# Two MLPs behind an attention: the work of the chunks issued piece by piece from tables, and a 4-byte tile made 64 bytes

## The chip, the core and the metric

The kernel runs on one NeuronCore of a Trainium2 chip. The metric is the device time of one execution in microseconds: the median of 3 runs is 816.31 us (815.45 to 816.59).

## What is computed

A masked attention (16 heads, 768 tokens, head size 64) gives x of 1536 tokens by 512 features. Two MLPs follow, and they are what the change touches:

```python
def _moe_ref(x, w_in, w_out):          # first layer, w_in 512 x 2048, w_out 2048 x 512
    h = x @ w_in
    g = h - np.tanh(h)
    return (g @ w_out).astype(np.float32)

def _moe2_ref(x, w_in, w_out):         # second layer, same sizes
    h = x @ w_in
    g = h * (1.0 / (1.0 + np.exp(-1.702 * h)))
    return (g @ w_out).astype(np.float32)
```

## The kernel before

Attention runs first (to about 257 us) and isn't changed. The MLPs work through 16 chunks, 8 for each layer; a chunk is 256 of the 2048 inner features, in two halves j = 0, 1 of 128. The 1536 tokens are three blocks t = 0, 1, 2 of 512. The weights come as 64-bit floats. For each half of a chunk `load_w` loads 1 MB into `raw` on SP's queue and makes 32-bit floats of it in steps: p1 (clip, L109), p2, p3, p4 (shifts and ors on the halves of the word, L114, L120, L126) and p5 (L135) on VectorE (DVE), q4 (L131) on ScalarE (ACT) between p4 and p5. `raw` and the result `w` have one buffer for each half j.

For precision each operand of a product is split into a high part, rounded by ACT (`wh` L141, `gh` L651, `xh`, `th`, `sh`), and a low rest, by GpSimd (POOL) or DVE (`wl` L144, `gl` L652, `xl`, `tl`, `sl`); a product is then three matmuls of 512 columns on TensorE (PE): high x high, high x low, low x high. "h" products (`h_mm`, 12 matmuls) make a unit (t, j) of the hidden layer from x; `act1` applies the activation (ACT, L642 or L645), the gate (DVE, L643 or L646) and splits the result into gh and gl. `out_mm` (12 matmuls for a unit, 3 for each quarter d of the output) multiplies by w_out and sums over both j in PSUM; `out_evac` adds the four quarters into `acc` (DVE, L692; in the first chunk of a layer a copy on ACT, L690), and after the last chunk of layer 1 splits them into the next layer's xh and xl (L695, L696), after the last of layer 2 stores them.

The first chunk of a layer, c = 0 and 8, is a `plain_chunk`: six h products, one for each unit. In the other 14, `strassen_chunk`, the units of t = 0, 1 are made by seven products P1 to P7 of 6 matmuls instead of four h of 12; t = 2 keeps h. They need sums of weights s1 to s4 (`s_sums`, POOL, L548, written into `ws` and split into sh, sl) and sums of tokens T1 to T4 (`t_sum`, DVE, L576, once a layer, split into th, tl, T4 into xh, xl of t = 1). P1, P6, P7, P4 go into one PSUM bank y, with copies `keep` to SBUF between them (p1, u2, u3, L633); P5 and P3 into a bank w. The results are added on DVE: x = P2 + p1 (L768), z = w + u3 (L784), w + u2 (L795).

All order is written out by hand (`manual_schedule`): the program's order is the order of each engine's queue, and an instruction that waits holds back what stands behind it on its engine. In a steady Strassen chunk PE runs P1, P2, out of (c-1, t 2, j 0), P6, P5, out of (c-1, 2, 1), P7, h20, P4, P3, out of (0,0), (0,1), h21, out of (1,1), (1,0).

Tiles in SBUF are placed pool by pool in steps of 32 bytes. The pool `op` holds acc2, th, tl and last `ready` (4 bytes for each partition); behind it come `sp` (sh, sl) and `gp` (f, gh, gl, and the sums t, u, p).

Of the kernel before, what the change touches and what calls it, by code (L numbers as in the profile page):

```python
# [57 lines left out]
def lsh_attention_then_two_mlps(  # L58
# [100 lines left out]

# [398 lines left out]
    def t_sum(n):  # L558
        b11, b21, b12, b22 = (
            [acc01[:, cc + 2 * i, t * TB : (t + 1) * TB] for cc in range(2)]  # L560
            for t in range(2)
            for i in range(2)
        )
        for cc in range(2):
            if n < 3:
                o = gp.tile([128, TB], F32, tag="u", name=f"t{n}_{cc}", bufs=4)
            else:
                o = acc2[:, 2 * (n - 3) + cc]
            tt[n, cc] = o
            a, b = {  # L570
                1: lambda: (b12, b11[cc]),
                2: lambda: (b22, tt[1, cc]),
                3: lambda: (b22, b12[cc]),
                4: lambda: (b21, tt[2, cc]),
            }[n]()
            nc.vector.tensor_tensor(o, a[cc], b, ALU.subtract)  # L576
# [54 lines left out]
    def keep(o, name):  # L631
        u = gp.tile([128, TB], F32, tag="u", name=name, bufs=4)
        nc.scalar.activation(u, o, AF.Copy)  # L633
        return u
# [3 lines left out]
    def act1(c, t, j, h, apart):  # L638
        f = gp.tile([128, TB], F32, tag="f", name=f"f{c}_{t}_{j}", bufs=3)
        g = f if apart else h  # L640
# [17 lines left out]
        return act2

    def out_mm(c, t, j, first, last):  # L660
        if first:
            oacc[t] = [
# [5 lines left out]
        for d in range(4):
            o = oacc[t][d // 2][:, d % 2, :]
            if c < LAYER:  # L670
                f = slice(512 + d * 128, 512 + (d + 1) * 128)
                prods = ((woh[:, f], hi), (woh[:, f], lo), (wol[:, f], hi))
            else:
                f = slice(d * 128, (d + 1) * 128)
                prods = (
                    (hi[:, f], woh[:, 512:]),
                    (hi[:, f], wol[:, 512:]),
                    (lo[:, f], woh[:, 512:]),
                )
            for n, (a, m) in enumerate(prods):  # L680
                nc.tensor.matmul(o, a, m, start=(first and n == 0), stop=(last and n == 2))  # L681

    def out_evac(c, t, ds=range(4)):
        tok = slice(t * TB, (t + 1) * TB)
        la, r = divmod(c, LAYER)
        for d in ds:
            o = oacc[t][d // 2][:, d % 2, :]
            m = acc_of(d, t)
            if r == 0:
                nc.scalar.activation(m, o, AF.Copy)  # L690
            else:
                nc.vector.tensor_tensor(m, o, m, ALU.add)  # L692
            if r == LAYER - 1:
                if la == 0:
                    nc.scalar.activation(xh[:, d, tok], m, AF.Copy)  # L695
                    nc.gpsimd.tensor_tensor(  # L696
                        xl[:, d, tok], m, xh[:, d, tok].bitcast(F32), ALU.subtract
                    )
                else:
                    r0 = t * TB + d * 128  # L700
                    nc.sync.dma_start(out=out[r0 : r0 + 128, :], in_=m)
        if 3 in ds:
            oacc.pop(t)

    def load(c, j):
        if c < NCHUNK:
            parts[c, j] = load_w(c, j)

    def part(c, j, *which):
        if c < NCHUNK:  # L710
            for n in which:
                if n == 7:
                    parts[c, j][7](slice(0, 512))
                elif n == 8:
                    parts[c, j][7](slice(512, 1024))
                else:
                    parts[c, j][n]()

    def plain_chunk(c):
        units = [(t, j) for t in range(NTB) for j in range(CH)]  # L720
        tags = ("T", "T", "v", "g")
        n1 = c + 1
        first = c == 0
        fill = (
            lambda: (t_sum(1), first or part(n1, 0, 0), first and load(c + 2, 0)),
            lambda: (t_sum(2), t_split(1, nc.gpsimd), first or part(n1, 0, 1)),
            lambda: (
                t_sum(3), t_sum(4), t_split(2, nc.gpsimd),
                part(n1, 1, 0, 1) if first else part(n1, 0, 2, 3),
            ),  # L730
            lambda: (
                first or (part(n1, 0, 4, 5), load(c + 2, 0)),
                part(n1, 1, 2, 3) if first else part(n1, 1, 0, 1),
                t_split(3, nc.gpsimd), part(n1, 0, 6, 7, 8),
            ),
            lambda: (first or part(n1, 1, 2, 3), t_split(4, nc.gpsimd)),
            lambda: (part(n1, 1, 6), s_sums(n1, 0), part(n1, 1, 8), load(c + 2, 1)),
        )
        for n in range(len(units)):
            t, j = units[n]  # L740
            if n < 2:
                h = h_mm(c, t, j, tags[n % 4])
                if c:
                    out_mm(c - 1, 2, n, n == 0, n == 1)
                    if n == 1:
                        out_evac(c - 1, 2)
            else:
                t, j = units[n - 2]
                out_mm(c, t, j, j == 0, j == CH - 1)
                if j == CH - 1:  # L750
                    out_evac(c, t)
                if n == 5:
                    part(n1, 1, 4, 5)
                t, j = units[n]
                h = h_mm(c, t, j, tags[n % 4])
            act1(c, t, j, h, n % 2 == 0)()
            fill[n]()
# [136 lines left out]
```

## Time and profile before

| | us |
|---|---|
| median of 3 runs | 816.31 (815.45 to 816.59) |
| the profiled execution | 816.48 |
| its span, first to last instruction | 814.7 |
| busy in it: PE, DVE, ACT, POOL | 778.3, 616.0, 419.4, 413.8 |
| mean granted clock of PE | 0.994 |

One execution is profiled; all rows below are from it. A timeline lists instructions by start and duration; "[0.23 <-ACT u L633]" means that the engine stood idle for 0.23 us until ACT's instruction on tile u, line 633, was through. Matmuls overlap in a pipeline, so from one to the next it is the distance of the starts that counts, not the duration.

### The profile page before, as it was taken

How to read it: one execution, taken by the hardware profiler on the slowest of the kernel's cores; microseconds unless marked ns; L12 is line 12 of the kernel's file. 1: busy time of each engine (PE TensorE's matmuls, PEld its weight loads, DVE VectorE, ACT ScalarE, POOL GpSimd, SP SyncE). 2: the span in 40 equal slices, each digit the busy share in tenths (PEclk: the TensorE clock that was granted, in tenths of full speed). 3: DMA queues.
4: the chain of work that ended last, by engine and by line, in shares of the span. 5: the costliest groups of instructions: out<-in, count | busy, mean ns of one | idle time of the engine just before them, and what ended most of it. 6: DMA issues, size and time to landing. Idle time of an engine off the chain costs nothing.

```text
span 814.7 us, 10025 instructions
## 1 busy us (share of the span) xinstructions
PE 778.3 (96%) x3708; PEld 565.8 (69%) x3708; DVE 616.0 (76%) x840; ACT 419.4 (51%) x793; POOL 413.8 (51%) x342
## 2 busy tenths in 40 slices
PE   5899999999999989999999999998899999999997
PEld 3566666666665867777777777776687777777775
DVE  4787877776764858779797797988688787887854
ACT  4777777767775455433444334545544344343440
POOL 5443444444112683645636446697746536456351
PEclk9999999999999999999999999999999999999999
DMA  9526214314102011211122111111211113111004
GB/s 262 180 74 207 108 49 156 130 37 145 72 1 104 1 52 55 101 52 52 51 68 89 52 52 56 60 41 52 90 66 51 52 52 103 52 51 52 2 1 154
DMA packets 12993, 62.89 MB, mean 77 GB/s; under 512 B 1616, under 2 KB 2512, under 8 KB 8848
## 3 DMA queue, kind: packets, MB, share of 16 engines
q1 hardware_dynamic: 8928, 46.21, 15.8%
q0 software_dynamic: 3872, 15.99, 6.8%
q8 instruction: 29, 0.48, 0.2%
q14 instruction: 20, 0.16, 0.1%
q10 hardware_dynamic: 144, 0.05, 0.0%
HBM read 59.10 MB, written 3.15 MB: 76 GB/s over the span
## 4 chain that ended last, share of the span: by engine, by line
DVE 36%; PE 33%; POOL 11%; ACT 11%; issue 6%; DMA 2%; DVEq 0%; POOLq 0%; ACTq 0%
PE pv L378 9%; PE tp L359 8%; PE sc L324 8%; DVE w L120 6%; DVE w L126 6%; DVE acc L692 5%; POOL w L548 5%; DVE w L114 4%; PE o L681 4%; DVE w L135 2%; ACT gh L651 2%; DVE gl L652 2%; ACT raw L131 2%; POOL sl L552 2%; POOL wl L144 2%
## 5 line engine op out<-in xcount | busy, mean ns | idle before, releaser
L652 POOL TENSOR_TENSOR gl<-f,gh 128x512 fp32r<-128x512 f32 x62 | 98.2, 1584 | 191.5 <-ACT gh L651 191.5
L692 DVE TENSOR_TENSOR acc<-o,acc 128x512 f32<-128x512 f32 x168 | 105.0, 678 | 6.2 <-PE o L681 6.0
L144 POOL TENSOR_TENSOR wl<-w,wh 128x512 fp32r<-128x512 f32 (+1 forms) x62 | 97.0, 1575 | 18.1 <-ACT wh L141 16.3
L131 ACT ACTIVATE raw<-raw 128x1024 f32<-128x1024 f32 x32 | 36.5, 1142 | 133.9 <-DVE w L126 130.1
L367 ACT ACTIVATE pt<-tp 128x384 f32<-128x384 f32 x184 | 80.3, 489 | 47.7 <-PE tp L359 46.8
L338 DVE TENSOR_REDUCE nm<-sc 128x1 f32<-128x768 f32 x96 | 91.5, 954 | 14.6 <-PE sc L324 13.4
L359 PEld LDWEIGHTS tp<-eye_sb,pr 128*128 128x128 f32 x576 | 61.6, 141 | 53.5 <-issue 25.7
L342 ACT ACTIVATE pr<-sc,nb 128x768 f32<-128x768 f32 x96 | 87.0, 906 | 16.6 <-DVE nb L340 8.9
L359 PE MATMUL tp<-eye_sb,pr 128*128 128x128 f32 x576 | 83.5, 281 | 0.0
L681 PE MATMUL o<-wh,gh 128*128 128x512 f32 x192 | 77.3, 403 | 5.2 <-ACT acc L690 2.6
L378 PE MATMUL pv<-pt,v 128*64 128x384 f32 x384 | 82.0, 510 | 0.0
L681 PE MATMUL o<-gl,wh 128*128 128x512 f32 x192 | 76.6, 399 | 2.3 <-DVE gl L652 1.3
L681 PE MATMUL o<-gh,wh 128*128 128x512 f32 x192 | 77.3, 403 | 0.9 <-DVE acc L692 0.9
L681 PE MATMUL o<-wh,gl 128*128 128x512 f32 x192 | 76.6, 399 | 0.4 <-POOL gl L652 0.4
L681 PE MATMUL o<-wl,gh 128*128 128x512 f32 x192 | 75.9, 395 | 0.0
L681 PE MATMUL o<-gh,wl 128*128 128x512 f32 x192 | 75.8, 395 | 0.0
L651 ACT ACTIVATE gh<-f 128x512 fp32r<-128x512 f32 x62 | 39.1, 630 | 47.4 <-DVE f L646 24.0
L593 PE MATMUL h<-xh,wh 128*128 128x512 f32 x160 | 63.3, 396 | 0.0
L593 PE MATMUL h<-xl,wh 128*128 128x512 f32 x160 | 63.2, 395 | 0.0
L593 PE MATMUL h<-xh,wl 128*128 128x512 f32 x160 | 62.9, 393 | 0.0
L324 PE MATMUL sc<-ka,qa 128*128 128x384 f32 x192 | 55.7, 371 | 3.1 <-DVE qa L228 2.6
L135 DVE SCALAR_TENSOR_TENSOR w<-raw,w 128x1024 f32<-128x1024 f32 x32 | 40.8, 1276 | 22.0 <-ACT raw L131 22.0
(145 smaller groups left out, 1677.3 us busy)
## 6 DMA issues: line engine op xcount, KB each, us to landing
raw<-in_w SPq DMA_DIRECT2D x32, 1024.0 KB, 4.8
ka<-in_kd POOLq DMA_DIRECT2D x7, 768.0 KB, 4.6
qa<-in_qd POOLq DMA_DIRECT2D x7, 768.0 KB, 6.6
r<-in_rr SPq DMA_DIRECT2D x7, 768.0 KB, 4.6
v<-in_vv SPq DMA_DIRECT2D x8, 384.0 KB, 3.1
out<-acc SPq DMA_DIRECT2D x12, 256.0 KB, 2.1
qb<-in_qd POOLq DMA_DIRECT2D x7, 384.0 KB, 7.9
r<-in_rr SPq DMA_DIRECT2D x2, 384.0 KB, 3.7
```

The source lines that it names most:

```text
L135: nc.vector.scalar_tensor_tensor(wf, sq, 1.0, wf, op0=ALU.is_ge, op1=ALU.mult)
L144: nc.gpsimd.tensor_tensor(wl[c, j][:, f], ws[c, j][:, f], wh[c, j][:, f].bitcast(F32), ALU.subtract)
L324: nc.tensor.matmul(sc[:, hf, :HALF], (qa, qb)[n][:, h, t0 : t0 + QT], (ka, kb)[n][:, h, hf * HALF : (hf + 1) * HALF], start=(n == 0), stop ...
L338: nc.vector.tensor_reduce(nm, sc[:, :, :HALF], AX.XY, ALU.max, negate=True)
L342: nc.scalar.activation(pr.rearrange("p (a b) -> p a b", a=2), sc[:, :, :HALF], AF.Exp, bias=nb, scale=D**-0.5, accum_out=sums[u][:, j, h : ...
L359: nc.tensor.transpose(tp[:, k * 128 : (k + 1) * 128], pr[:, c * 128 : (c + 1) * 128], eye_sb)
L367: nc.scalar.activation(dst, src, AF.Copy)
L378: nc.tensor.matmul(acc[u][h * 64 : (h + 1) * 64, :UT], v[:, h, c, :], probT[u][:, c, h, :], start=(c == 0), stop=(c == NCH - 1),)
L593: nc.tensor.matmul(o, a, b, start=(start and n == 0 and m == 0), stop=(n == len(pairs) - 1 and m == 2), skip_group_check=not start,)
L652: (nc.gpsimd if apart else nc.vector).tensor_tensor(lo, g, hi.bitcast(F32), ALU.subtract)
L681: nc.tensor.matmul(o, a, m, start=(first and n == 0), stop=(last and n == 2))
L692: nc.vector.tensor_tensor(m, o, m, ALU.add)
```

## The change

`plain_chunk`, `strassen_chunk` and their helpers with several steps in one are replaced by single steps and a table of names for each chunk, which `issue` runs in order. A name is a step and its indices: P1 to P7 a product, `h20` the h product of t 2, j 0, `o210` quarter d 0 of out of (2, 1), `ev10` the evacuation of quarter 0 of t 1, `t00`, `g00`, `hi00`, `lo00` activation, gate and split of a unit, `kp1`, `ku2`, `ku3` the copies, `xadd`, `zadd`, `wadd` the sums, `p11` to `p51`, `q41`, `whi1`, `wloa1`, `wlob1` the conversions of half 1, `ld1` its load, `s1`, `shi12`, `slo12` the weights' sums, `ts10`, `th10`, `tl10` the tokens'. "-" behind a name means the chunk before, "+" the next, "++" the one behind it. Chunks 0, 1, 7, 8, 9 and the end have tables of their own (those of 1 and 9 are left out here), all others run STEADY. `ready`, which serves one small instruction at the change of layers, is made 64 bytes for each partition instead of 4.

```diff
@@ load_w
+        parts["p1", c, j] = p1
...
+        parts["hi", c, j] = hi_part
+        parts["loa", c, j] = lambda: lo_part(slice(0, 512))
+        parts["lob", c, j] = lambda: lo_part(slice(512, 1024))
@@ the tiles of the MLPs
-    ready = op.tile([128, 1], F32, name="ready")
+    ready = op.tile([128, 16], F32, name="ready")
@@ s_sums, t_sum, t_split, act1 and out_evac become
+    def s_sum(c, n):
...
+    def s_hi(c, n):
...
+    def s_lo(c, n):
...
+    def t_sum(c, n, cc):
...
+    def t_hi(n, cc):
...
+    def t_lo(n, cc):
...
+    def act(c, t, j):
...
+    def gate(c, t, j):
...
+    def g_hi(c, t, j):
...
+    def g_lo(c, t, j):
...
+        eng = nc.gpsimd if apart(c, t, j) else nc.vector
...
+    def out_mm(c, t, j, d):
...
+    def evac(c, t, d):
...
+    def x_hi(t, d):
...
+    def x_lo(t, d):
...
@@ plain_chunk and strassen_chunk become
+    def keep(c, n, o):
+        us[c, n] = gp.tile([128, TB], F32, tag="u", name=f"u{c}_{n}", bufs=4)
+        nc.scalar.activation(us[c, n], o, AF.Copy)
+    def product(c, n):
+        if n == 1:
+            yw[c, 0] = bank("v", f"y{c}")
+        elif n == 2:
+            hp[c, 0, 0] = bank("T", f"x{c}")
+        elif n == 5:
+            yw[c, 1] = bank("g", f"w{c}")
+        elif n == 4:
+            hp[c, 0, 1] = yw[c, 0]
+        s_mm(hp[c, 0, 0] if n == 2 else yw[c, n in (3, 5)], c, n, n in (1, 2, 5))
+    def add(c, n):
+        if n == "x":
+            o, a, b = hp[c, 0, 0], hp[c, 0, 0], us[c, 1]
+        elif n == "z":
+            o, a, b = hp[c, 1, 1], yw[c, 1], us[c, 3] = bank("T", f"z{c}"), yw[c, 1], us[c, 3]
+        else:
+            o, a, b = hp[c, 1, 0], yw[c, 1], us[c, 2] = yw[c, 1], yw[c, 1], us[c, 2]
+        nc.vector.tensor_tensor(o, a, b, ALU.add)
+    def issue(name, c):
+        kind = name.rstrip("0123456789")
+        n = [int(x) for x in name[len(kind) :]]
+        if name[:2] in ("p1", "p2", "p3", "p4", "q4", "p5"):
+            parts[name[:2], c, n[-1]]()
+        elif kind == "ld":
+            load_w(c, n[0])
+        elif kind in ("whi", "wloa", "wlob"):
+            parts[kind[1:], c, n[0]]()
+        elif kind == "s":
+            s_sum(c, n[0])
+        elif kind in ("shi", "slo"):
+            (s_hi if kind == "shi" else s_lo)(c, n[0] // 2)
+        elif kind == "ts":
+            t_sum(c, *n)
+        elif kind in ("th", "tl"):
+            (t_hi if kind == "th" else t_lo)(*n)
+        elif kind == "P":
+            product(c, n[0])
+        elif kind in ("kp", "ku"):
+            keep(c, n[0], yw[c, 0])
+        elif kind in ("xadd", "zadd", "wadd"):
+            add(c, kind[0])
+        elif kind == "h":
+            t, j = n
+            tag = "T" if c % LAYER or t != 1 else "vg"[j]
+            hp[c, t, j] = bank(tag, f"h{c}_{t}_{j}")
+            h_mm(c, t, j, hp[c, t, j])
+        elif kind == "t":
+            act(c, *n)
+        elif kind == "g":
+            gate(c, *n)
+        elif kind in ("hi", "lo"):
+            (g_hi if kind == "hi" else g_lo)(c, *n)
+        elif kind == "o":
+            out_mm(c, *n)
+        elif kind == "ev":
+            evac(c, *n)
+        elif kind in ("xh", "xl"):
+            (x_hi if kind == "xh" else x_lo)(*n)
+        elif kind == "tab":
             nc.scalar.activation(ready, ready, AF.Sigmoid)
+    STEADY = (
+        "P1 g21- hi21- s4 shi12 ev10- ev11- P2 p11+ shi34 slo34 slo12 ev12- o200- ev13- "
+        "o201- o202- kp1 xadd o203- p20+ t00 g00 p21+ p30+ P6 p40+ p31+ lo21- P5 o210- "
+        "o211- ku2 q40+ o212- o213- P7 p50+ ev21- ev22- ku3 hi00 zadd lo00 whi0+ h20 P4 "
+        "ev23- ld0++ wloa0+ t11 wlob0+ P3 ev20- t20 t01 g20 g11 g01 hi11 hi01 lo11 o000 "
+        "o001 wadd t10 o002 hi20 o003 lo01 o010 p41+ o011 o012 g10 o013 ev01 q41+ lo20 "
+        "h21 p51+ ev00 s1+ hi10 s2+ ev02 ev03 whi1+ o110 lo10 p10++ o111 o112 o113 o100 "
+        "t21 wlob1+ o101 s3+ o102 o103 wloa1+ ld1++ "
+    )
+    ORDER = {
+        0: (
+            "whi0+ ts31 ts10 h00 ts30 wloa0+ ld1+ h01 h11 t00 ts11 t01 wlob0+ h10 ts20 "
+            "g00 hi00 th20 lo00 ts40 g01 ts21 hi01 o000 lo01 ts41 o001 th10 th30 th21 "
+            "o002 o003 h20 t11 o010 p11+ t10 th11 p21+ o011 tl10 g10 th31 tl20 hi10 h21 "
+            "o012 p31+ ld0++ o013 p41+ ev01 t20 g11 g20 tl30 ev00 lo10 p10++ q41+ tl21 "
+            "ev02 hi20 t21 p51+ tl31 th40 lo20 ev03 hi11 s1+ lo11 P1+ whi1+ s2+ P2+ ld1++ "
+            "th41 o100 o101 o102 o103 wlob1+ shi12+ o110 o111 kp1+ o112 s3+ slo12+ o113 "
+            "ev10 ev11 P6+ g21 s4+ "
+        ),
...
+        7: (
+            "g21- P1 P2 s4 shi12 p11+ shi34 kp1 slo12 ev11- P5 ev12- P6 ku2 ev10- slo34 "
+            "ev13- hi21- p20+ xadd o200- P7 t00 p30+ lo21- ku3 o201- o202- o203- p21+ P4 "
+            "p40+ q40+ o210- g00 zadd p31+ p50+ t01 p41+ o211- t11 g01 ev20- hi00 h20 "
+            "whi0+ hi01 lo00 wlob0+ t20 g11 o212- wloa0+ hi11 ev21- ld0++ lo11 o213- g20 "
+            "o000 ev22- ev23- q41+ hi20 P3 lo01 wadd p51+ t10 p10++ p20++ g10 o001 whi1+ "
+            "lo20 o002 hi10 o003 wlob1+ o010 o011 o012 o013 ev01 ev00 h21 ev03 lo10 o110 "
+            "xh01 xh00 wloa1+ xl01 ev02 o111 t21 xh03 o112 g21 xl00 o113 xh02 o100 o101 "
+            "p30++ hi21 ev10 o102 o103 xl03 ev11 o200 xh11 xl02 o201 ts10+ ts11+ xh10 "
+            "th10+ h00+ ev13 xh13 ev12 lo21 "
+        ),
+        8: (
+            "ld1+ o202- o203- p11+ tl10 tab o210- t00 p21+ o211- g00 o212- o213- p40+ "
+            "ts20 ev22- ev20- xh12- xl11- xl10- h01 xl12- ev21- xl13- h11 ts21 hi00 xh22- "
+            "xh20- ev23- xh21- q40+ xh23- t01 p50+ g01 whi0+ lo00 o000 h10 xl22- hi01 "
+            "xl21- xl23- ts31 lo01 xl20- ts41 t10 g10 p31+ ts40 th21 hi10 wlob0+ o001 "
+            "tl21 t11 wloa0+ th11 h20 p41+ o002 o003 q41+ ts30 o010 o011 ev00 th20 p51+ "
+            "ld0++ t20 g11 lo10 h21 o012 t21 ev01 tl20 o013 ev03 g20 hi11 o100 o101 P2+ "
+            "s1+ ev02 whi1+ hi20 tl11 P1+ s2+ o102 wlob1+ o103 shi12+ th40 g21 lo11 th41 "
+            "hi21 o110 kp1+ th31 o111 s3+ o112 s4+ ev10 shi34+ xadd+ slo12+ P6+ o113 "
+        ),
...
+        NCHUNK: (
+            "ev10- ev11- ev12- ev13- g21- hi21- o200- o201- o202- o203- lo21- o210- o211- "
+            "o212- o213- ev20- ev21- ev22- ev23- "
+        ),
+    }
+    for c in range(NCHUNK + 1):
+        for name in ORDER.get(c, STEADY).split():
+            at = c + name.count("+") - name.count("-")
+            if at < NCHUNK:
+                issue(name.strip("+-"), at)
```

## Rows read from the trace of the kernel before

**Rows 1.** The page, busy time of each engine over the whole span

```profile
PE 778.3 (96%) x3708; PEld 565.8 (69%) x3708; DVE 616.0 (76%) x840; ACT 419.4 (51%) x793; POOL 413.8 (51%) x342
```

**Rows 2.** Timeline of PE: start us, duration us, line, output<-streamed operand, weights

```profile
257.07 0.50 PE L593 MATMUL h<-xh,wh 128*128 128x512 f32 x1
...
258.79 0.39 PE L593 MATMUL h<-xl,wh 128*128 128x512 f32 x1
...
262.42 0.39 PE L593 MATMUL h<-xh,wl 128*128 128x512 f32 x1
...
418.55 0.39 PE L681 MATMUL o<-gl,wh 128*128 128x512 f32 x1
...
423.68 0.39 PE L681 MATMUL o<-gh,wl 128*128 128x512 f32 x1
...
711.29 0.40 PE L593 MATMUL y<-th,sh 128*128 128x512 f32 x1
...
713.39 0.40 PE L681 MATMUL o<-wh,gh 128*128 128x512 f32 x1
...
809.87 0.39 PE L681 MATMUL o<-wh,gl 128*128 128x512 f32 x1
```

**Rows 3.** Timeline of PE, one steady chunk, [idle before <-releaser]

```profile
398.83 0.40 PE L681 MATMUL o<-gh,wh 128*128 128x512 f32 x1
...
406.15 0.50 PE L593 MATMUL y<-xh,wh 128*128 128x512 f32 x1 [0.23 <-ACT u L633]
...
412.63 0.50 PE L681 MATMUL o<-gl,wh 128*128 128x512 f32 x1 [0.21 <-DVE gl L652]
...
432.48 0.39 PE L681 MATMUL o<-gh,wh 128*128 128x512 f32 x1
```

**Rows 4.** Timeline of PE, P6's first matmul in chunks 1 and 9

```profile
294.90 0.50 PE L593 MATMUL y<-th,sh 128*128 128x512 f32 x1 [3.18 <-ACT p L633]
...
575.79 0.50 PE L593 MATMUL y<-th,sh 128*128 128x512 f32 x1 [3.90 <-ACT p L633]
```

**Rows 5.** A stage: length, busy PE, PEld, DVE, ACT, POOL, clock, DMA

```profile
524.00:591.00 67.00, 57.78 (x230) 44.69 (x229) 51.11 (x47) 37.43 (x62) 53.58 (x36) 0.95 0.17 62
```

**Rows 6.** Timelines of DVE and ACT, the same chunk

```profile
402.25 2.20 DVE L126 SCALAR_TENSOR_TENSOR w<-raw,w 128x1024 uint32<-128x1024 uint32 x1
...
404.49 1.13 ACT L131 ACTIVATE raw<-raw 128x1024 f32<-128x1024 f32 x1 [3.72 <-DVE w L126]
...
405.51 0.59 ACT L633 ACTIVATE u<-y 128x512 f32<-128x512 f32 x1
...
420.52 1.23 DVE L126 SCALAR_TENSOR_TENSOR w<-raw,w 128x1024 uint32<-128x1024 uint32 x1
```

**Rows 7.** Groups by line and shape, 330 to 815: busy us, mean ns | idle

```profile
L652 POOL TENSOR_TENSOR gl<-f,gh 128x512 fp32r<-128x512 f32 x55 | 87.3, 1588 | 172.3 <-ACT gh L651 172.3
...
L120 DVE SCALAR_TENSOR_TENSOR w<-raw,w 128x1024 uint32<-128x1024 uint32 x26 | 46.0, 1768 | 0.4
...
L126 DVE SCALAR_TENSOR_TENSOR w<-raw,w 128x1024 uint32<-128x1024 uint32 x26 | 45.5, 1751 | 0.9
...
L114 DVE TENSOR_SCALAR w<-raw 128x1024 uint32<-128x1024 uint32 x26 | 33.2, 1277 | 19.5 <-POOL w L548 19.0
...
L135 DVE SCALAR_TENSOR_TENSOR w<-raw,w 128x1024 f32<-128x1024 f32 x26 | 32.8, 1261 | 16.1 <-ACT raw L131 16.1
...
L109 DVE TENSOR_SCALAR raw<-raw 128x1024 f32<-128x1024 f32 x25 | 23.6, 945 | 0.0
```

**Rows 8.** Timeline of DVE, the same chunk

```profile
399.85 2.37 DVE L120 SCALAR_TENSOR_TENSOR w<-raw,w 128x1024 uint32<-128x1024 uint32 x1
...
414.59 1.77 DVE L114 TENSOR_SCALAR w<-raw 128x1024 uint32<-128x1024 uint32 x1
...
416.88 2.47 DVE L692 TENSOR_TENSOR acc<-o,acc 128x512 f32<-128x512 f32 x4
```

**Rows 9.** DMA issues, 300 to 815: KB each, median us to landing

```profile
raw<-in_w SPq DMA_DIRECT2D x26, 1024.0 KB, 4.8
```

More of the change, by code (lines that the diff above doesn't have):

```diff
@@ L540, in s_sums, with s_part @@
         s1, s2, s3, s4 = w0[:, 512:768], w0[:, 768:], w1[:, 512:768], w1[:, 768:]
-        if n == 0:
+        o, a, b, f = {
+            1: (s1, a21, a22, ALU.add),
+            2: (s2, s1, a11, ALU.subtract),
+            3: (s3, a11, a21, ALU.subtract),
+            4: (s4, a12, s2, ALU.subtract),
+        }[n]
+        nc.gpsimd.tensor_tensor(o, a, b, f)
+    def s_part(c, n):
+        return (x[c][:, 2 * n : 2 * n + 2].rearrange("p a b -> p (a b)") for x in (sh, sl))
+    def s_hi(c, n):
+        if c not in sh:
@@ L551, in s_sums @@
-        nc.scalar.activation(h, w, AF.Copy)
-        nc.gpsimd.tensor_tensor(l, w, h.bitcast(F32), ALU.subtract)
-    tt = {}
[L558 to L576, printed above, removed]
@@ new lines, in lsh_attention_then_two_mlps @@
+    tt = {}
+    def t_sum(c, n, cc):
+        b11, b21, b12, b22 = (
+            acc01[:, cc + 2 * i, t * TB : (t + 1) * TB] for t in range(2) for i in range(2)
+        )
+        if n < 3:
+            o = gp.tile([128, TB], F32, tag="u", name=f"t{c}_{n}_{cc}", bufs=4)
+        else:
+            o = acc2[:, 2 * (n - 3) + cc]
+        tt[n, cc] = o
+        a, b = {
+            1: lambda: (b12, b11),
+            2: lambda: (b22, tt[1, cc]),
+            3: lambda: (b22, b12),
+            4: lambda: (b21, tt[2, cc]),
+        }[n]()
+        nc.vector.tensor_tensor(o, a, b, ALU.subtract)
@@ L629, in s_mm, with apart @@
         products(o, [(a(kc), b(kc)) for kc in range(2)], start)
[L631 to L640, printed above, removed]
+    def apart(c, t, j):
+        return t == j or t == 2 if c % LAYER else j == 0
+    fs = {}
+    def act(c, t, j):
+        f = fs[c, t, j] = gp.tile([128, TB], F32, tag="f", name=f"f{c}_{t}_{j}", bufs=3)
@@ L658, in act1 @@
[L658 to L662, printed above, removed]
+            nc.scalar.activation(f, hp[c, t, j], AF.Tanh)
+        else:
+            nc.scalar.activation(f, hp[c, t, j], AF.Sigmoid, scale=1.702)
+    def gate(c, t, j):
+        h, f = hp.pop((c, t, j)), fs.pop((c, t, j))
+        g = fs[c, t, j] = f if apart(c, t, j) else h
+        nc.vector.tensor_tensor(g, h, f, ALU.subtract if c < LAYER else ALU.mult)
+    def g_hi(c, t, j):
+        gh[c, t, j] = gp.tile([128, TB], F32R, tag=f"gh{t}{j}", name=f"gh{c}_{t}_{j}")
+        nc.scalar.activation(gh[c, t, j], fs[c, t, j], AF.Copy)
@@ L663, in out_mm @@
+    def g_lo(c, t, j):
+        gl[c, t, j] = gp.tile([128, TB], F32R, tag=f"gl{t}{j}", name=f"gl{c}_{t}_{j}")
+        eng = nc.gpsimd if apart(c, t, j) else nc.vector
+        eng.tensor_tensor(
+            gl[c, t, j], fs.pop((c, t, j)), gh[c, t, j].bitcast(F32), ALU.subtract
+        )
+    def out_mm(c, t, j, d):
+        first = j == (1 if t == 1 and c % LAYER else 0)
+        if first and d == 0:
+            oacc[c, t] = [
                 ps.tile([128, 2, 512], F32, tag="S", name=f"o{c}_{t}_{i}", bufs=2)
@@ L665, in out_mm @@
             ]
-        hi, lo = gh.pop((c, t, j)), gl.pop((c, t, j))
+        hi, lo = gh[c, t, j], gl[c, t, j]
         woh, wol = wh[c, j], wl[c, j]
[L668 to L681, printed above, removed]
@@ L683, in out_evac @@
-    def out_evac(c, t, ds=range(4)):
-        tok = slice(t * TB, (t + 1) * TB)
[L685 to L757, printed above, removed]
@@ L822, in lsh_attention_then_two_mlps @@
-    load(1, 1)
-    for c in range(NCHUNK):
-        (strassen_chunk if c % LAYER else plain_chunk)(c)
-    out_mm(NCHUNK - 1, 2, 0, True, False)
-    out_mm(NCHUNK - 1, 2, 1, False, True)
-    out_evac(NCHUNK - 1, 2)
+        o = oacc[c, t][d // 2][:, d % 2, :]
+        if c < LAYER:
+            f = slice(512 + d * 128, 512 + (d + 1) * 128)
+            prods = ((woh[:, f], hi), (woh[:, f], lo), (wol[:, f], hi))
+        else:
+            f = slice(d * 128, (d + 1) * 128)
+            prods = (
+                (hi[:, f], woh[:, 512:]),
+                (hi[:, f], wol[:, 512:]),
+                (lo[:, f], woh[:, 512:]),
+            )
@@ new lines, in out_mm @@
+        for n, (a, m) in enumerate(prods):
+            nc.tensor.matmul(o, a, m, start=(first and n == 0), stop=(not first and n == 2))
+    def evac(c, t, d):
+        o = oacc[c, t][d // 2][:, d % 2, :]
+        m = acc_of(d, t)
+        if c % LAYER == 0:
+            nc.scalar.activation(m, o, AF.Copy)
+        else:
+            nc.vector.tensor_tensor(m, o, m, ALU.add)
+        if c == NCHUNK - 1:
+            r0 = t * TB + d * 128
+            nc.sync.dma_start(out=out[r0 : r0 + 128, :], in_=m)
```

123 lines of the change are left out of this document (31 added, 92 removed), and 16 rows, old and new, of the table ORDER.

## The prediction

> **What bounds the kernel now.** I read the busy shares of the page first: TensorE (PE) 96%, VectorE (DVE) 76%, ScalarE (ACT) and GpSimd (POOL) 51% [rows 1]. So an edit can pay only where PE waits or where one matmul takes longer than it must. The change leaves attention alone, so the part that counts runs from the first h matmul at 257.07 us to the end of the last out matmul, 809.87 + 0.23 us: 553.0 us [rows 2]. By the code it holds 2220 matmuls of 512 columns: 160 x 3 of h_mm, 14 x 42 of s_mm, 16 x 72 of out_mm.
>
> The second view is the start-to-start time of matmuls in stretches without waits. Here there are two paces, not one. Where both operands are xh, xl, wh or wl, 16 steps take 262.42 - 258.79 = 3.63 us, 0.2268 us each. In an out_mm run, which streams gh and gl past wh, 22 steps take 5.13 us, 0.2332 each. In P6 and P5, which stream th and tl past the weights sh and sl, 9 steps take 2.10 us, 0.2333 each [rows 2]. The slow kinds are out_mm (1152) and P3, P5, P6 and P7 (14 x 24 = 336), 1488 in all. In each, exactly one operand comes from the pools sp or gp. In the program every tile is placed in steps of 32 bytes, so `ready` takes 32, and all of sp and gp, which come behind it, start 32 bytes past a multiple of 64; xh, xl, wh, wl, th and tl start on one. A difference of 6.4 ns is 15 columns at the fast pace's 0.427 ns per column, about one more piece of 64 bytes. That the start is the cause is an inference: it fits both ways round (streamed operand in the first layer, weights in the second and in P6), and no row takes it alone.
>
> With these paces the 2220 matmuls need 1488 x 0.2332 + 732 x 0.2268 = 347.0 + 166.0 = 513.0 us. PE therefore loses 553.0 - 513.0 = 40.0 us to waits. The third view, PE's timeline, says where. A steady Strassen chunk lasts 432.48 - 398.83 = 33.65 us, against 96 x 0.2332 + 42 x 0.2268 = 31.9 for its 138 matmuls: 1.74 lost, of which the rows show P4 waiting for `u` and out for `gl` [rows 3]. Times 14 chunks, 24.4. The other 15.6 lie in the two seams: at chunk 0 to 1 PE stands 3.18 us before P6; in the seam of the layers 3.90 at the same place, and the stage from 524 to 591 runs at a mean granted clock of 0.95 [rows 4, 5].
>
> **The change part by part.**
>
> The 64-byte tile moves sp and gp onto multiples of 64. Cost: nothing, one memset of 16 values instead of one, in DVE's idle time before the first gate. Gain: bounded by 0 and by 1488 x 0.0064 = 9.5 us. I take 9.5, because the form nearest in kind, P2 (same helper, six matmuls to a bank) with aligned weights, is in the fast class and P6 is not. The Trainium skill, page "SBUF — State Buffer", section "Specifications (TRN2)", gives lines of 16 bytes and a penalty for each cross to a new line. A start at 32 is on such a line already, so by that page of the Trainium skill the new start would bring nothing and the sum would end 9.5 us higher. The two paces in the rows speak against that as the whole story.
>
> The helpers are cut into pieces (one sum, one conversion, one evacuation at a time). By count nothing is added or removed: the same 2220 matmuls, sums, splits, evacuations and loads. What moves is the place of each in its engine's queue; every queue runs in program order.
>
> Steady chunks (STEADY, chunks 2 to 6 and 10 to 15): PE's own order is the old one. With 0.2268 per matmul PE's due times from the chunk's start are P1 0, P2 1.4, out(2,0) 2.7, P6 5.4, P5 6.8, out(2,1) 8.2, P7 10.9, h20 12.2, P4 15.0, P3 16.3, out(0,0) 17.7, out(0,1) 20.4, h21 23.1, out(1,1) 25.9, out(1,0) 28.6, end 31.3. Against these I laid the other queues by hand:
> - P4 now waits because `q4` stands ahead of the copy `u3` on ACT and itself waits for `p4` on DVE: p4 ends at 404.45, q4 starts at 404.49, u3 at 405.51, P4 at 406.15 [rows 3, 6]. In the table s3 is summed a chunk earlier, so `p2` no longer waits long for POOL, and q4 comes between u2 and u3. DVE reaches p4 by 8 to 12, q4 ends by 13, u3 runs at 12.5 to 13.6, before 15.0. Gone.
> - `slo12` now ends just after P6 has started; in the table it is ready near 3.2 for 5.4. Gone.
> - `zadd` needs u3 (13.1) and has to end before P3 (16.3). Behind g00 DVE has p21, p30, p40, p31, p50 and two evacuations: at the mean times 1.28 + 1.77 + 1.75 + 1.77 + 1.26 + 1.24 = 9.1 us [rows 7, 8], from 5.0 to 14.1. So zadd is through at 14.8. Cover 1.5.
> - `lo01` stands at the end of the chain P4, t01, g01, hi01, P3, wadd, lo01: six hops of 0.6 to 0.7 and the handovers from 16.3 end near 20.1; out(0,1) wants it at 20.4 and its second matmul at 20.6. Cover 0.3 to 0.5, the thinnest.
> - out(1,1) wants ev00 and ev01 (25.2 for 25.9), out(1,0) wants lo10 (27 for 28.6). Covered.
>
> I leave 0.3 us per chunk for the thin places: 14 x 0.3 = 4.2.
>
> Seam 0 to 1: three h products now run before the first out, P6 comes behind both outs of chunk 0, T1 to T4 are spread over DVE, ACT and POOL. POOL's queue (wl halves, lo, tl, s, slo; 1.59 is the mean of a lo [rows 7]) reaches slo12 at 28 to 29 after the start, for P6 at 29.9; slo34 follows near 33.8, for P7 at 33.3. I leave 1.0 of the old 4.7, most of which was the 3.18 before P6.
>
> Seam of the layers: the first h of layer 2 starts after xl00 to xl03 with out(7,2,0) half done, the rest of out(7,2) covers xl10 to xl13, and tl30 to tl41 go to chunk 9. The order is sound, but POOL becomes the bound: it was busy 53.6 us in the stage from 524 to 591 [rows 5], and the 230 matmuls of that stage need only 230 x 0.2268 = 52.2. Some of POOL's work can move into the chunks on both sides, and DVE's contended operations are no lighter. I leave 5.0 of about 11.
>
> End: g21 now comes behind ev10 to ev13 of chunk 15, so lo21 is ready some 3.6 us after out(1,0) for a matmul due at 3.2: 0.5. The last two evacuations and the store stay. A few slower matmuls after each wait that remains: 1.0.
>
> **How the numbers follow.** New length: 2220 x 0.2268 = 503.5, plus 4.2 + 1.0 + 5.0 + 0.5 + 1.0 = 11.7, gives 515.2 against 553.0: 37.8 less. The profiled execution took 816.48 us (its span 814.7 and 1.8 around it), 0.2 above the median of 816.31. Forecast 816.3 - 37.8 = 778.5. Floor of it (no wait left): 766.8.
>
> **Rivals.**
> 1. The start address is not the cause, or only where gp's tiles are streamed (first layer's out, 8 x 72 = 576 matmuls). For: no row isolates it, and the weights are read while the matmul before still runs. Then 9.5, or 9.5 x 912/1488 = 5.8, is missing: 784 to 788. The Trainium skill's lines of 16 bytes ("SBUF — State Buffer", "Specifications (TRN2)") lead to the first of the two.
> 2. DVE is late inside a chunk. The conversions cost 1.2 us alone and 2.2 to 2.4 beside POOL [rows 6, 8]; at the upper times the chain to zadd takes 1.77 + 2.37 + 2.20 + 2.37 + 2.20 + 1.24 = 12.2 instead of 9.1 and P3 waits 1.5 to 2. Against: between slo12, lo21 (near 5) and lo00 (13.7) POOL is idle. Half of it, 1 us x 14, gives 792; all of it 806.
> 3. Slower than before: the reload loop. `raw` and `w` have one buffer for each half. The table issues the load of half 1 after p51, at the chunk's end, and puts p11 of the next chunk five DVE operations into that chunk, where before it came in the middle. From p11 round to p51 DVE has 9 conversions and 16 operations of 0.62 [rows 8], plus q41 (1.14) and the landing (4.8) [rows 9]: with the mean times 0.95 + 2 x (1.28 + 1.77 + 1.75 + 1.26) = 13.1, and 13.1 + 9.9 + 1.1 + 4.8 = 28.9, which 31.3 covers. If every conversion met POOL, 3 x 1.77 + 2 x (2.37 + 2.20 + 2.20) = 18.9 and the loop is 34.7, longer than the chunk is now (33.65): + 13 over 14 chunks, and with the seams' gain mostly eaten by the same queue about 820. It decides from a mean conversion of 2.0 us against 1.45 now. Against: POOL is busy only about half of a chunk.
> 4. The order does nothing and the wait moves (P4's to P3's, chunk for chunk), and the start does nothing: 816.
>
> **Chances.** Forecast (768 to 786) 0.62. Rival 1 with the order as forecast 0.15. Rival 2, with or without the pace, 0.17. Rival 3 0.04. Rival 4 0.02. The low end is the floor, a little over it; the high end takes in rival 1 and the mild half of rival 2: 768 to 795. A measurement of this kernel tells 0.2% (1.6 us) from no change. Faster 0.94, same 0.02, slower 0.04.
>
> **What would show it.** Pace: out runs and P5 to P7 at 0.227 per matmul, in both layers. Order: steady chunks of 31.3 to 31.9 us from P1 to P1, no idle of PE before P4, and what is left before P3 or the first gl of out(0,1). Seam: P6 of chunks 1 and 9 without a gap, POOL busy without a break from chunk 7's end to chunk 9, and h10, h20 or P6 waiting for xl or slo there. Rival 3: DVE idle ahead of p11, ended by the load. It is wrong if a new wait of over 1 us repeats in every chunk, or if the out runs keep 0.233.

## The result and the profile after

The changed kernel takes 780.12 us (780.07 to 780.75, 4 runs) against 816.39 before: a ratio of 0.956 (95% interval 0.9543 to 0.9576), 36.3 us less. The forecast was 778.5. The two terms of its sum, however, were both off, in opposite directions, and the runs below take them apart.

The page of the changed kernel: busy time of each engine [rows 1], then the chain that ended last, by engine.

```profile
PE 759.0 (97%) x3708; PEld 570.3 (73%) x3708; DVE 581.9 (75%) x840; ACT 424.5 (55%) x793; POOL 399.4 (51%) x342
...
PE 88%; DVE 3%; issue 2%; POOL 2%; DMA 2%; ACT 1%; POOLq 0%; DVEq 0%; ACTq 0%
```

By the chain, 88% of the span is now PE's own work. PE's timeline in a steady chunk, from P1 to the next P1, with the last matmul of h20 and the first of P4 [rows 3], then P6's first matmul in chunks 1 and 9 with the one before it [rows 4]:

```profile
412.40 0.40 PE L610 MATMUL y<-xh,wh 128*128 128x512 f32 x1
...
427.45 0.39 PE L610 MATMUL h<-xh,wl 128*128 128x512 f32 x1
427.68 0.39 PE L610 MATMUL y<-xh,wh 128*128 128x512 f32 x1
...
444.19 0.40 PE L610 MATMUL y<-xh,wh 128*128 128x512 f32 x1
...
287.68 0.40 PE L699 MATMUL o<-gh,wl 128*128 128x512 f32 x1
287.92 0.39 PE L610 MATMUL y<-th,sh 128*128 128x512 f32 x1
...
580.72 0.39 PE L699 MATMUL o<-wh,gl 128*128 128x512 f32 x1
580.95 0.40 PE L610 MATMUL y<-th,sh 128*128 128x512 f32 x1
```

The chunk lasts 31.79 us instead of 33.65 (32.00 in the second layer). P4 follows h20 after 0.23 us, one plain step, and P6 no longer waits in either place. The idle times of PE of more than 0.15 us in the MLPs are three, 1.5 us together:

```profile
527.06 0.50 PE L610 MATMUL h<-xl,wh 128*128 128x512 f32 x1 [0.34 <-POOL xl L722]
...
537.44 0.50 PE L699 MATMUL o<-wh,gh 128*128 128x512 f32 x1 [0.64 <-ACT acc L705]
...
771.57 0.50 PE L699 MATMUL o<-wh,gl 128*128 128x512 f32 x1 [0.48 <-POOL gl L672]
```

Before, the wait of 3.90 us in the seam of the layers [rows 4] was followed by slow matmuls:

```profile
577.11 0.63 PE L593 MATMUL y<-th,sh 128*128 128x512 f32 x1
...
579.67 0.63 PE L593 MATMUL w<-th,sh 128*128 128x512 f32 x1
```

Six steps take 2.56 us here, 0.43 each, at the lower of the clock's two levels, 1.2 GHz; the mean granted clock from 576 to 580 us was 0.61. In this seam 14 steps were of this length, seven here and seven behind an earlier wait, some 3 us more than at the usual 0.23. After the change none is, and from 520 to 600 us the granted clock is 1.00.

The pace [rows 2] is read from two runs of 24 out matmuls without a wait, one in each layer:

```profile
398.65 0.40 PE L699 MATMUL o<-gh,wh 128*128 128x512 f32 x1
...
403.94 0.39 PE L699 MATMUL o<-gh,wl 128*128 128x512 f32 x1
...
665.81 0.40 PE L699 MATMUL o<-wh,gh 128*128 128x512 f32 x1
...
671.18 0.39 PE L699 MATMUL o<-wh,gl 128*128 128x512 f32 x1
```

In the first layer 23 steps take 5.29 us, 0.2300 each, a little under the 0.2332 of before. In the second they take 5.37, 0.2335 each: nothing gained. Some groups of DVE and POOL [rows 7] have a shorter mean, though the instructions are the same:

```profile
L672 POOL TENSOR_TENSOR gl<-f,gh 128x512 fp32r<-128x512 f32 x55 | 76.4, 1390 | 158.5 <-ACT gh L667 153.1 <-PE w L610 5.5
...
L126 DVE SCALAR_TENSOR_TENSOR w<-raw,w 128x1024 uint32<-128x1024 uint32 x25 | 32.6, 1304 | 0.3
...
L120 DVE SCALAR_TENSOR_TENSOR w<-raw,w 128x1024 uint32<-128x1024 uint32 x24 | 31.8, 1326 | 0.0
...
L114 DVE TENSOR_SCALAR w<-raw 128x1024 uint32<-128x1024 uint32 x24 | 19.3, 805 | 0.3
```

A p3 takes 1.33 us on the mean instead of 1.77, a p4 1.30 instead of 1.75, a p2 0.81 instead of 1.28: these conversions now stand where POOL is mostly idle. An instruction of POOL ran beside 70% of p3's time before and 20% after, 69 and 36% of p4's, 55 and 25% of p2's. p1 went the other way, from 50 to 95% and from 0.95 to 1.07 us.

### The profile page after: what moved, and what is told of

Same layout as the page of the kernel before. It is cut to its first block, busy times and chain, and to the rows that moved or that the text cites. A ratio compares the mean times of both kernels' runs of the same rounds, so it can differ in the third digit from the quotient of the medians.

```text
span 778.6 us, 10045 instructions
## 1 busy us (share of the span) xinstructions
PE 759.0 (97%) x3708; PEld 570.3 (73%) x3708; DVE 581.9 (75%) x840; ACT 424.5 (55%) x793; POOL 399.4 (51%) x342
## 4 chain that ended last, share of the span: by engine, by line
PE 88%; DVE 3%; issue 2%; POOL 2%; DMA 2%; ACT 1%; POOLq 0%; DVEq 0%; ACTq 0%
PE o L699 31%; PE h L610 12%; PE y L610 10%; PE pv L386 9%; PE tp L367 9%; PE sc L332 8%; PE w L610 5%; PE x L610 2%; DMA ka<-in_kd 1%; DMA r<-in_rr 1%; POOL xl L722 1%; PE rb L411 1%; PE pb L260 1%; PE po L291 1%; DVE acc L590 1%
## 5 line engine op out<-in xcount | busy, mean ns | idle before, releaser
L672 POOL TENSOR_TENSOR gl<-f,gh 128x512 fp32r<-128x512 f32 x62 | 86.0, 1387 | 171.0 <-ACT gh L667 165.5
L707 DVE TENSOR_TENSOR acc<-o,acc 128x512 f32<-128x512 f32 x168 | 108.8, 684 | 54.5 <-PE o L699 53.7
L144 POOL TENSOR_TENSOR wl<-w,wh 128x512 fp32r<-128x512 f32 (+1 forms) x62 | 85.7, 1393 | 18.9 <-ACT wh L141 18.9
L731 ACT ACTIVATE u<-y 128x512 f32<-128x512 f32 x42 | 25.2, 601 | 107.9 <-PE y L610 107.9
L667 ACT ACTIVATE gh<-f 128x512 fp32r<-128x512 f32 x62 | 39.1, 630 | 28.3 <-DVE f L663 28.1
L332 PE MATMUL sc<-kb,qb 128*128 128x384 f32 x192 | 50.2, 342 | 2.0 <-DVE qb L298 2.0
```

The lines of the kernel that those rows point to most:

```text
L144: nc.gpsimd.tensor_tensor(wl[c, j][:, f], ws[c, j][:, f], wh[c, j][:, f].bitcast(F32), ALU.subtract)
L332: nc.tensor.matmul(sc[:, hf, :HALF], (qa, qb)[n][:, h, t0 : t0 + QT], (ka, kb)[n][:, h, hf * HALF : (hf + 1) * HALF], start=(n == 0), stop ...
L667: nc.scalar.activation(gh[c, t, j], fs[c, t, j], AF.Copy)
L672: eng.tensor_tensor(gl[c, t, j], fs.pop((c, t, j)), gh[c, t, j].bitcast(F32), ALU.subtract)
```

## The experiments: the tile

**Undo the tile alone**, the order stays:

```diff
-    ready = op.tile([128, 16], F32, name="ready")
+    ready = op.tile([128, 1], F32, name="ready")
```

> The order of the tables with the 4-byte tile, so that sp and gp start 32 bytes past a multiple of 64 again. Theory A (the start of a tile sets the pace of matmuls): the first layer's out products, which stream gh and gl and run at 0.229 to 0.232 us in the changed kernel, go back to 0.2332; 576 of them by 2.5 ns are 1.4 us, 781.5. Rival B (the pace is set by something other than the start, the new order is all of the gain): 780.1 and the same paces as in the changed kernel.

Measured: 781.4 us (ratio to before 0.9588, 0.9574 to 0.9602). The run of 24 in the first layer:

```profile
399.05 0.40 PE L699 MATMUL o<-gh,wh 128*128 128x512 f32 x1
...
404.42 0.40 PE L699 MATMUL o<-gh,wl 128*128 128x512 f32 x1
```

5.37 us, 0.2335 each. So the 64-byte tile is worth about 1.3 of the 36.3 us, nearly all of it in the first layer's out; the second layer runs at 0.233 with either. The order is worth the other 35.

**Do the tile alone**, the order of before:

> The order of before with the 64-byte tile. Theory A: the first layer's out products drop from 0.2332 to 0.229 to 0.231; as PE also waits in every chunk, less than 1.5 us of it reaches the end, 815 to 816. Rival B: 816.4 and 0.2332. By the forecast on record, in which all 1488 products with an operand from sp or gp get the fast pace, it would have been up to 9.5 us faster, 807.

Measured: 816.13 us, ratio 1.0007 (0.9998 to 1.0017): no change. The first layer's out does run at 0.2303 on the mean instead of 0.2331, but what the products lose PE waits longer.

**128 bytes:**

```diff
-    ready = op.tile([128, 16], F32, name="ready")
+    ready = op.tile([128, 32], F32, name="ready")
```

> The changed kernel with the tile made 128 bytes, so that sp and gp start on multiples of 128, as xh, xl, wh and wl do. Theory A2 (weights want a start on 128, streamed operands gain from 64 on): all products go to 0.2268, 2220 by 4.2 ns are 9.3 us, 771. Theory A (64 is all there is): 780.1 and the second layer's out, P3 and P5 to P7 stay at 0.2333. Rival C (weights from sp and gp are slow for where they lie, not how they start): 778 to 780, with the first layer's out at 0.2268 at most.

Measured: 780.07 us. A start on 128 does nothing for the weights, and the first layer's out lost part of what 64 had given (5.35 us for 23 steps):

```profile
397.93 0.39 PE L699 MATMUL o<-gh,wh 128*128 128x512 f32 x1
...
403.28 0.39 PE L699 MATMUL o<-gh,wl 128*128 128x512 f32 x1
```

So a start on a multiple of 64, the theory of the forecast, is not enough, and a rounder start does not help further. A pattern is left: by the sizes of the tiles in the kernel, all operands of the fast products (xh, xl, wh, wl) lie whole multiples of 256 bytes apart. With a tile of 4, 64 or 128 bytes sp and gp lie 32, 64 or 128 bytes off that grid.

**512 and 256 bytes**, which put sp and gp on the grid of the others:

```diff
-    ready = op.tile([128, 16], F32, name="ready")
+    ready = op.tile([128, 128], F32, name="ready")      # 512; [128, 64] for 256
```

> The changed kernel with the tile made 512 bytes. The runs so far: sp and gp shifted by 32 bytes gives 0.2333 in the first layer's out, by 64 0.2307, by 128 0.2327; products of xh, xl with wh, wl take 0.2285 (0.2268 in long runs), and those tiles lie at 128 from a multiple of 512, all of them. Theory D (what counts is the shift of the streamed operand against the weights, modulo 512 or less, not a start on 64 or 128): at a shift of 512 every product runs as xh with wh do, 1475 products by 3 to 6 ns, 4.5 to 9 us less, 771 to 776. Theory C (tiles far up in SBUF, or written just before, are slow wherever they start): 780 and 0.2327 to 0.2333 for the second layer's out.

> The changed kernel with the tile made 256 bytes. Theory D with a period of 256: as with 512, 771 to 776. With a period of 512: between, or as slow as with 128, 780. Theory C: 780.

Measured: 771.24 us (ratio 0.9453, 0.9439 to 0.9467) and 771.45 (0.9458, 0.9444 to 0.9472). Timeline of PE with 512 bytes, the two runs of out, then P5's first matmul in two steady chunks:

```profile
395.95 0.39 PE L699 MATMUL o<-gh,wh 128*128 128x512 f32 x1
...
401.16 0.39 PE L699 MATMUL o<-gh,wl 128*128 128x512 f32 x1
...
658.66 0.39 PE L699 MATMUL o<-wh,gh 128*128 128x512 f32 x1
...
663.87 0.39 PE L699 MATMUL o<-wh,gl 128*128 128x512 f32 x1
...
385.07 0.39 PE L610 MATMUL w<-th,sh 128*128 128x512 f32 x1
...
416.35 0.39 PE L610 MATMUL w<-th,sh 128*128 128x512 f32 x1
```

Both runs take 5.21 us, 0.2265 each, and the chunk takes 31.28, which is 138 x 0.2267: PE does nothing but matmuls, at one pace. This is the effect for which the forecast had 9.5 us, from 4 bytes to 64. From 64 bytes it measures 780.1 - 771.2 = 8.9; from 4 bytes it is 10.0 with 256 (781.4 - 771.45) and 10.2 with 512.

**Start or distance?** A 32-byte tile ahead of all others, besides the 256 bytes:

```diff
+    pad = xpool.tile([128, 8], F32, name="pad")
+    nc.vector.memset(pad, 0.0)
     xh = xpool.tile([128, NCC, NT], F32R, name="xh")
```

> As with the 256-byte tile, and a 32-byte tile (filled once with zeros) placed ahead of all others, so that xh, xl, wh, wl, th, tl, sp and gp all start 160 past a multiple of 256 instead of 128: no start is kept, every distance is. If the distance of the streamed operand from the weights, modulo 256, sets the pace: 0.2268 everywhere, 771.4. If it is the start itself (128 modulo 256 fast, other starts slow): 0.2307 to 0.2333 in all products, h too, 780 to 786.

Measured: 771.21 us. The first layer's run of 24:

```profile
395.80 0.39 PE L701 MATMUL o<-gh,wh 128*128 128x512 f32 x1
...
401.01 0.39 PE L701 MATMUL o<-gh,wl 128*128 128x512 f32 x1
```

5.21 us again, with all these tiles moved by 32 bytes, the move that gives 0.2335 when sp and gp make it alone. So it is not the start itself. What matters is how far the streamed operand and the weights lie apart, modulo 256: at 0 every product is fast. The size of the distance is not all, though: with 64 bytes the first layer streams an operand 64 above its weights (0.2300), the second one 64 below (0.2335).

**The pace in the old order:**

```diff
-    ready = op.tile([128, 1], F32, name="ready")
+    ready = op.tile([128, 64], F32, name="ready")
```

> The order of before with the 256-byte tile. All products at 0.2268: 1488 by 6.4 ns are 9.5 us. If PE sets the length of a chunk also in the old order, all of it reaches the end: 806.5. If the chain of conversions on DVE and POOL sets it (the steady chunk's 33.65 stays), only the seams and the end gain, some 240 products, 1 to 3 us: 813 to 815, and PE's waits grow by what the products lose.

Measured: 814.85 us, ratio 0.9988 (0.9979 to 0.9997). P5's first matmul in two steady chunks:

```profile
396.70 0.40 PE L593 MATMUL w<-th,sh 128*128 128x512 f32 x1
...
430.31 0.40 PE L593 MATMUL w<-th,sh 128*128 128x512 f32 x1
```

33.61 us against 33.65: the chunk stays as long as it was, although its matmuls now need 31.3. Over the MLPs the matmuls need some 8 us less and PE waits some 7 us longer. So in the old order another engine's chain set the length of a chunk, not PE. From 4 to 256 bytes the pace is worth 1.3 us there (816.11 in the runs beside it, to 814.85) and 10.0 in the new order (781.4 to 771.45).

## The experiments: the order

**s3 and s4 back in their own chunk**, the first half of the forecast's explanation of P4's wait (shown for chunks 3 to 5 and 11 to 15; chunks 2, 6 and 10 have the half of it that goes with their neighbours' tables):

```diff
-        "P1 g21- hi21- s4 shi12 ev10- ev11- P2 p11+ shi34 slo34 slo12 ev12- o200- ev13- "
-        "o201- o202- kp1 xadd o203- p20+ t00 g00 p21+ p30+ P6
+        "P1 g21- hi21- shi12 ev10- ev11- P2 p11+ slo12 ev12- o200- ev13- "
+        "o201- o202- kp1 xadd o203- t00 g00 s3 s4 shi34 slo34 p20+ p21+ p30+ P6
...
-        "t21 wlob1+ o101 s3+ o102 o103 wloa1+ ld1++ "
+        "t21 wlob1+ o101 o102 o103 wloa1+ ld1++ "
```

> The changed kernel with s3 and s4 of the steady chunks back behind g00 in their own chunk, as before, so that p2 of the next chunk waits for POOL again and p4, q4 and u3 come later. If this place was what made P4 wait: PE idles 0.3 to 0.6 us before P4 or P7 in chunks 3 to 6 and 11 to 15, 3 to 6 us in all, 783 to 786. If the other moves (q4 between u2 and u3, the conversions spread out) cover it alone: 780 to 781.

Measured: 780.04 us, no change. Timeline of ACT in one chunk, q4 and u3 in the changed kernel and then in this one:

```profile
420.53 1.16 ACT L131 ACTIVATE raw<-raw 128x1024 f32<-128x1024 f32 x1 [0.40 <-DVE w L126]
...
425.13 0.60 ACT L731 ACTIVATE u<-y 128x512 f32<-128x512 f32 x1 [3.43 <-PE y L610]
```

```profile
422.86 1.17 ACT L131 ACTIVATE raw<-raw 128x1024 f32<-128x1024 f32 x1 [3.20 <-DVE w L126]
...
424.65 0.60 ACT L731 ACTIVATE u<-y 128x512 f32<-128x512 f32 x1 [0.62 <-PE y L610]
```

The chunk in which these stand begins with P1 at 412.40 and at 411.93. q4 starts 8.1 us after that in the one and 10.9 in the other, and u3 12.7 after it in both: it waits for P7 (y), not for q4. Before, q4 started 404.49 - 390.26 = 14.2 after P1 (P1's first matmul stood at 390.26) [rows 6]. So P4 goes without a wait whether s3 and s4 stand in the old place or the new. The old state is not back, however. POOL's s3 and s4 before, then in this run, and DVE's two p2 in this run:

```profile
397.67 0.73 POOL L548 TENSOR_TENSOR w<-w,w 128x256 f32<-128x256 f32 x1
398.36 0.74 POOL L548 TENSOR_TENSOR w<-w 128x256 f32<-128x256 f32 x1
...
410.95 0.74 POOL L555 TENSOR_TENSOR w<-w,w 128x256 f32<-128x256 f32 x1
411.65 0.74 POOL L555 TENSOR_TENSOR w<-w 128x256 f32<-128x256 f32 x1
...
417.00 3.42 DVE L114 TENSOR_SCALAR w<-raw 128x1024 uint32<-128x1024 uint32 x2
```

Before, POOL came to s3 7.4 us after P1, and p2 waited for POOL, 19.0 us in all [rows 7]. Here half 1 is converted early, POOL comes to s3 1.0 us ahead of P1, and no p2 waits; the two p2 only take 1.7 us each. So the expectation's "p2 of the next chunk waits for POOL again" did not come about, and whether that wait was what delayed P4 stays untested. The other half of the forecast's reason, q4 between u2 and u3, names no change: ACT had u2 at 400.19, q4 at 404.49 and u3 at 405.51 before too [rows 6].

**p3 and p4 of half 1 back behind the evacuations of t 0**, as before, and with them q4, p5, the high part, the weights' sums and the next load (hi10 moves ahead of them):

```diff
-        "o201- o202- kp1 xadd o203- p20+ t00 g00 p21+ p30+ P6 p40+ p31+ lo21- P5 o210- "
+        "o201- o202- kp1 xadd o203- p20+ t00 g00 p21+ p30+ P6 p40+ lo21- P5 o210- "
...
-        "o001 wadd t10 o002 hi20 o003 lo01 o010 p41+ o011 o012 g10 o013 ev01 q41+ lo20 "
-        "h21 p51+ ev00 s1+ hi10 s2+ ev02 ev03 whi1+ o110 lo10 p10++ o111 o112 o113 o100 "
+        "o001 wadd t10 o002 hi20 o003 lo01 o010 o011 o012 g10 o013 hi10 ev01 ev00 ev02 ev03 "
+        "p31+ lo10 p41+ q41+ lo20 h21 p51+ s1+ s2+ whi1+ o110 p10++ o111 o112 o113 o100 "
```

> The changed kernel with p3 and p4 of half 1 in the steady chunks put back behind the evacuations of t 0, as before, and q4, p5, the weights' sums and the reload after them. Theory (the early conversion of half 1 is what freed slo12, p2, p4, q4 and u3 of the next chunk): whi1, s1, s2 and slo12 come 3 to 4 us later, P6 waits for slo or P4 for u3 by 0.3 to 1.5 us in each of 11 chunks, 783 to 796; p11 then also waits for the load issued after p51. Rival (the spread of the other steps covers it, as it covered s3 and s4): 780 to 781.

Measured: 806.64 us, ratio to before 0.9892 (0.9876 to 0.9909): 26.5 us of the 36.3 are gone again, and the time is 10.6 above the upper end of what was expected. The waits of this kernel over the MLPs (us in total, times, longest), then P5's first matmul in two steady chunks, and DVE's wait at p1:

```profile
PEld o L699 <- DVE acc L707: 15.0, 11, 1.8
...
DVE raw L109 <- DMA raw<-in_w: 14.1, 9, 2.5
...
PEld y L610 <- POOL sl L569: 9.5, 9, 1.8
```

```profile
392.48 0.40 PE L610 MATMUL w<-th,sh 128*128 128x512 f32 x1
...
426.67 0.40 PE L610 MATMUL w<-th,sh 128*128 128x512 f32 x1
...
420.73 0.99 DVE L109 TENSOR_SCALAR raw<-raw 128x1024 f32<-128x1024 f32 x1 [1.41 <-DMA raw<-in_w]
```

A chunk takes 34.19 us, 2.40 more than in the changed kernel and more than the 33.65 of before. PE loses them in two places: 0.8 us at P6, since half 1 converted late makes s1, s2 and slo12 late, and 1.6 at out(2,0), since the load that may start only after p51 is late for p11, behind which the evacuations that out(2,0) needs stand on DVE. p2 waits for POOL again (11.4 us, 8 times). The second place is the link of the forecast's rival 3, the reload, but not by its cause: rival 3 asked for a mean conversion of 2.0 us, and here the nine of a chunk take 1.2 on the mean (p3 1.32, p4 1.30, p2 1.19). So it is the place in the queue that costs. It is not the order of before either: there p11 stood some 23 us into the chunk, just ahead of the p2 at 414.59 [rows 8], here it stays near the chunk's start. The 26.5 us are the price of the late half 1 within the new order, not what its early place gained over the old one.

**The end**, besides the 256 bytes:

```diff
-            "ev10- ev11- ev12- ev13- g21- hi21- o200- o201- o202- o203- lo21- o210- o211- "
+            "ev10- ev11- g21- hi21- lo21- ev12- ev13- o200- o201- o202- o203- o210- o211- "
```

> The 256-byte tile with the new order, and at the end g21, hi21, lo21 of chunk 15 ahead of ev12 and ev13: the wait of the last out for lo21 (0.65 us) goes, 770.8; if ev12 and ev13 become late for o202 instead, 771.4.

Measured: 771.03 us (ratio 0.9448, 0.9435 to 0.9461). The wait for lo21 is gone from the timeline, and a wait of 0.14 us for an evacuation has come; against 771.24 and 771.45 the intervals overlap, so that the worth of this edit can't be told from nothing. Its median is the lowest of all, 9.1 us below the changed kernel, nearly all of it the tile's doing.

## Why the prediction was right, and where it was not

**The total** was 37.8 us of gain, measured 36.3. With the mean steps of each kind, the matmuls of the MLPs alone account for 514.4 us before and 513.0 after, and the waits for 38.6 and 3.5. So the pace gave 1.4 instead of 9.5 us and the waits 35.1 instead of 28.3 (40.0 to 11.7). Two misses of 8.1 and 6.8 us nearly cancelled: that the total came within 1.6 us was luck in good part.

**The pace: the step that failed** is the start on a multiple of 64, reached by way of "about one more piece of 64 bytes", and the 9.5 us taken from it. Its arithmetic was off too: 0.2268 us for 512 columns are 0.443 ns a column, not 0.427, so that 6.4 ns are 14.4 columns or 58 bytes. That the place of sp and gp makes their products slow was right: 256 bytes bring all of them to 0.2267. That a multiple of 64 would do it was not, and the forecast's own sign of being wrong, "if the out runs keep 0.233", came true in the second layer (0.2335). The forecast had a chance of 0.15 for this rival, with 784 to 788; only the better order kept the time below.

The Trainium skill's page "SBUF — State Buffer", section "Specifications (TRN2)", gives lines of 16 bytes and a penalty for each cross to a new line. By that page of the Trainium skill alone a move from 32 to 64 would gain nothing, as both lie on such a line. The first layer disagrees mildly (0.2335 to 0.2300), and the move from 64 to 256, again from line to line, gives 8.9 us; so lines of 16 bytes are not what the two paces come from.

**The waits were mis-sized to the safe side.** For the steady chunks 0.3 us each was left; they have none (31.79 us in the first layer, all of it matmuls). The cover at zadd and lo01 was worked out with the conversions' means of before. In the new order p3 and p4 are a quarter shorter and p2 over a third, so DVE had more room than the sum gave it. In the seam of the layers 5.0 us were left on the ground that POOL becomes the bound; the two waits there are 0.34 and 0.64 us of idle time. In the seam of chunk 0 nothing is left of the 1.0; four h products run ahead of the first out there, not three. The end was right: 0.5 forecast, 0.48 seen, for lo21 as named. One sum of the rivals was off: 34.7 - 33.65 over 14 chunks is 14.7, not 13.

Where the time went can be read off the two timelines, from the first matmul of P2 in one chunk to that in another, in us. The forecast's share of the waits, without the pace, stands beside it (3.7 and 6 for the seams, 1.74 - 0.3 for each Strassen chunk, less the 1.5 left for the end and for slower matmuls, which stands in the last row):

| stretch | before | after | gain | forecast's waits |
|---|---|---|---|---|
| first h to chunk 2 | 67.28 | 60.89 | 6.4 | 5.1 |
| chunk 2 to 7, steady | 168.30 | 158.94 | 9.4 | 7.2 |
| chunk 7 to 10, the layers' seam | 112.99 | 99.42 | 13.6 | 8.9 |
| chunk 10 to 15, steady | 167.85 | 160.00 | 7.9 | 7.2 |
| chunk 15 to the last matmul | 36.38 | 36.98 | -0.6 | -0.1 |

The gain of the waits was missed most in the seam of the layers, and some 3 of its 13.6 us are the slow clock behind the old wait, which is gone with it.

**P4's wait** went, as forecast; why is not settled. The place of s3 and s4 is not needed for it. p2 no longer waits for POOL, as the forecast said, but it is half 1's early conversion that lets POOL come to s3 and s4 in time: with s3 and s4 put back p2 did not wait, with half 1 late it did. Whether P4 would wait again if p2 did, or whether the earlier p1 of half 0 and the shorter p3 and p4 cover that too, no run shows by itself. Without the early half 1 the new order loses 26.5 us; the forecast had no line for it, and named one of the two links by which it is lost, the reload, as rival 3 at a chance of 0.04.

**Open:** why the distance modulo 256 matters (whether the two reads of PE meet in the memory, and how the 0.2300 at +64 comes about) no run here shows. Distances of 32, 64, 128, 256 and 512 were tried. In the order only two moves of the steady chunks and one at the end were undone or tried alone; the tables of the seams were not, so that their share is read off the timelines and which of their moves earned it is open.

## What to carry to other kernels

Before an order is changed, ask in each stage whether PE or a chain through the other engines sets its length: the same faster matmuls were worth 1.3 us under the chain and 10.0 without it. With single buffers the step that frees a buffer decides (here p51 for the reload), and here it paid to have the conversions in stretches in which POOL is idle (p3 1.33 us instead of 1.77). A step that is put back in the program's order need not come back in time: look at the trace whether the old wait is there again before an undo is read as a test of it. Where matmuls of one shape show two paces, compare the addresses of the two operands modulo 256 and try one small tile ahead of a pool; a padding that was only tried at one size proves little either way.

## What the runs showed of the hardware

In runs of 24 out products the step between float32r matmuls of 512 columns is 0.2265 us when streamed operand and weights lie a multiple of 256 bytes apart in each partition (256 and 512 tried). In the first layer, where the streamed operand lies above the weights, it is 0.2335 at 32, 0.2300 at 64 and 0.2326 at 128; in the second layer, with the streamed operand 64 below, it is 0.2335. Moving all these tiles together by 32 bytes changed nothing. After a run of the slow kind the next fast products also began slowly: in the changed kernel the first seven steps take 0.229 to 0.234 us on the mean, and 0.2267 from the eleventh on; h takes 0.2288 on the mean there, and 0.2268 once all lie on one grid.
